# Five landing places instead of three for the second MLP's raw weights, and a later split of its first input block

## Chip, cores and metric

The program runs on one core of one Trainium2 chip. The metric is the device time of one execution in microseconds. Engines are named as in the profile: PE is TensorE (PEld its weight loads), DVE is VectorE, ACT is ScalarE, POOL is GpSimd, SP is SyncE, which issues all the transfers spoken of here.

## What is computed

Attention with a relative-position bias (four batches, eight heads, 576 positions, head dimension 64), then two MLPs on the resulting 2304 rows of 512:

```python
attn = softmax(q @ k.T / 8 + bias)                     # bias from a small MLP of the positions
x    = (attn @ v) as 2304 x 512
h    = max(x @ w1, x @ w2, x @ w3);  x = h @ w_out      # first MLP, hidden size 768
h    = x @ w_in                                         # second MLP, hidden size 2048
g    = h where h >= 1, 0 where h <= -1, (h + 1)**2 / 4 between
out  = g @ w_out
```

## The kernel before

Matrix products are made with each operand split into a high and a low fp16 part and three products of the parts. The program is one long Python loop; a scheduler at compile time puts each engine's instructions into a fixed order, by their place in the program and by when it thinks them ready. On the chip each engine then runs its list in order and waits where data isn't there. The same holds for SP's list of transfers.

The stretch of interest is the end of the attention and what follows it. At the end of the attention loop 45 units of the first MLP are still waiting in a list, `mlp_q` (L879, run at L1017): one last product of an earlier block (`mlp2`), then 18 `mlp1` and 4 `mlp2` of the block whose input lies in the tile "masks", then 18 `mlp1` and 4 `mlp2` of the last block, whose input lies in "xT". A unit `mlp1` (L800) is 12 matmuls (L808), a drain by ACT (L813) or DVE (L815), and for every third unit a split of the result by ACT (L819) and POOL (L820). A unit `mlp2` (L822) is 18 matmuls (L830), drains by ACT (L835) and a store to DRAM (L837). The first MLP's weights lie in `aw`, in the order in which the units use them: units 23 to 26 are the last to read its first 4096 columns.

Between these units stand the second MLP's raw weights: 32 pieces of 512 KB, each of which is loaded as it comes (L450), decoded into fp32 by ACT (L462, L463, L465) and DVE (L464), scaled by a maximum that PE helps to find (L549, L552), and split into two fp16 parts by ACT (L157) and DVE (L158) in its home. Pieces go by pairs; ten are done during the attention, the other 22 beside the 45 units, one pair for every four units (L1022). ACT's L462 or L463 is what reads a landing place last. A piece lands in one of three places in turn: before, `raws[0]`, `raws[1]` (the two halves of the first 2048 words of the tile `ws`) and `rt_` (the next 1024 words); from piece 12 on the first two are replaced by tiles named "v", of which there are two and which the attention also uses for its values. `load(2 * y + 2)` stands ahead of the decoding of pair y and `load(2 * y + 3)` behind it, in `late_pieces` (L556). The homes of the pieces are a list (L525); pieces 20 and 21 have theirs in "masks", so they wait for the block that reads it, pieces 22 to 26 in the last part of `ws`, 27 to 31 in tiles "k".

The second MLP takes its input in five blocks. `fetch_x2` (L851) brings a block into `qz`, `split_x2` (L855) finds its scale and splits it into one of two stores in turn, `x2_s` (L535): `ws`' first 4096 fp16 columns, which are `raws`, and `aw`'s first 4096. Block 0 is split behind unit 12 of `mlp_q`, counted from 0 (`PRM["xs"]`, L1019), block 1 during the second MLP's first block. That first block makes products L1056, results by ACT and DVE (L1069 to L1074) and products L1082, and needs the scales of all 32 pieces (`scales`, L1027). Beside it POOL combines weights for the later blocks (`wcomb`, L1111: L1120 to L1126, with ACT's L1125 between), which run with products L1134 and L1173 only.

Of the kernel before, what the change touches and what calls it, by code (L numbers as in the profile page):

```python
# [7 lines left out]
F16 = mybir.dt.float16  # L8
# [3 lines left out]
I64 = mybir.dt.int64  # L12
# [8 lines left out]
def kernel(ctx: ExitStack, tc: tile.TileContext, qt, kt, vr, small, mw1, mw2, mw3, mwo, win, wo2, out):  # L21
# [8 lines left out]
    P = 128  # L30
# [32 lines left out]
        group=16,  # L63
        look=4,
        xat=1,
        xs=12,
        bufs={'k': 5, 'pt': 4, 'xT': 2, 'phl': 4},
        xeng='vvvv',
        b1='vg',
# [23 lines left out]
    def st(shape, dt, tag):  # L93
        return sb.tile(shape, dt, tag=tag, name=tag, bufs=BUFS.get(tag, 1))
# [69 lines left out]
    if True:  # L164
# [361 lines left out]
        N_BIAS = 10  # L526
# [5 lines left out]
                home.append((st([P, S], F32, "k").bitcast(F16) if len(home) < 32 else st([P, 9, P], F16, "pt").rearrange("p c k -> p (c k)"))[:, :1024])  # L532
            return home[x]

        x2_s = [wss[:, 0:4], aws[:, 0:4]]  # L535
        n_late = [0]

        def late_to(n):
# [17 lines left out]
        def late_pieces():  # L556

            spec = []
            for ft in range(0, NF2, 2):
                spec.append([win[:, P * f:P * f + P].rearrange("(k p) f -> p k f", p=P) for f in (ft, ft + 1)])  # L560
                spec.append([wo2[P * f:P * f + P, :] for f in (ft, ft + 1)])

            spec = sum(spec, [])

            def load(x):
                if x >= len(spec):
                    return
                r = [raws[:, 0], raws[:, 1], rt_.rearrange("p a c -> p (a c)").bitcast(I64)][x % 3]
                if x >= N_BIAS + 2 and x % 3 < 2:
                    r = st([P, 10, 256], F16, "v").rearrange("p a c -> p (a c)")[:, 0:2048].bitcast(I64)  # L570
                loaded.append(raw_load(spec[x], r))

            loaded = []
            load(0)
            load(1)
            for y in range(len(spec) // 2):
                load(2 * y + 2)
                dst = [late_home(2 * y + i) for i in range(2)]
                zs = [decode(loaded[2 * y + i], st([P, S], F32, "sp")[:, :512].bitcast(U32), dst[i].bitcast(U32)) for i in range(2)]
                load(2 * y + 3)  # L580
                q = y // 2
                s = c_sq2[:, q:q + 1] if y % 2 else c_sp[:, 2 * q:2 * q + 2]
                pair_scale(s, [d.bitcast(U32) for d in dst], 12 if y % 2 else 14)
                for i in range(2):
                    split(dst[i][:, 0:512], dst[i][:, 512:1024], zs[i], s[:, 0:1] if y % 2 else s[:, i:i + 1], PENG[y % 2])
                yield
                yield
# [685 lines left out]
```

## Time and profile before

| | us |
|---|---|
| median of 3 runs | 1004.85 |
| lowest and highest | 1003.17, 1009.06 |
| the profiled execution | 1001.5 |
| its span (first to last instruction) | 999.6 |

The page gives the busy time of each engine over the span; the views used below are the busy time by stretches, the instructions of one engine in order of time, the waits of SP's queue, and the instructions of one line. In rows in order of time the bracket at the end gives the idle time just before the row and what ended it; "x12" is the number of instructions merged in the row.

### The profile page before, as it was taken

How to read it: one execution, taken by the hardware profiler on the slowest of the kernel's cores; microseconds unless marked ns; L12 is line 12 of the kernel's file. 1: busy time of each engine (PE TensorE's matmuls, PEld its weight loads, DVE VectorE, ACT ScalarE, POOL GpSimd, SP SyncE). 2: the span in 40 equal slices, each digit the busy share in tenths (PEclk: the TensorE clock that was granted, in tenths of full speed). 3: DMA queues.
4: the chain of work that ended last, by engine and by line, in shares of the span. 5: the costliest groups of instructions: out<-in, count | busy, mean ns of one | idle time of the engine just before them, and what ended most of it. 6: DMA issues, size and time to landing. Idle time of an engine off the chain costs nothing. (4 is left out here: it accounts for less than half of the span.)

```text
span 999.6 us, 25925 instructions
## 1 busy us (share of the span) xinstructions
PE 927.2 (93%) x10258; PEld 756.0 (76%) x10258; DVE 689.0 (69%) x1512; ACT 599.2 (60%) x1194; POOL 514.1 (51%) x734
## 2 busy tenths in 40 slices
PE   6768988899999999999899899999999999999996
PEld 5546777688888878778678778543688888888885
DVE  8998886767656686566454577876477586686565
ACT  3789875856665645778577698633444454454442
POOL 4133496748767755646367103995143344343442
PEclk8777979899999999999999999999999999999999
DMA  9996997997999879999989663010110010000000
GB/s 289 266 261 161 271 220 210 232 247 168 218 237 206 178 178 212 218 230 225 216 172 210 193 202 106 22 43 1 43 44 23 1 43 23 2 22 23 1 23 22
DMA packets 238969, 141.46 MB, mean 142 GB/s; under 512 B 187520, under 2 KB 217728, under 8 KB 238336
## 3 DMA queue, kind: packets, MB, share of 16 engines
q1 hardware_dynamic: 238688, 139.55, 58.6%
q8 instruction: 80, 1.31, 0.5%
q14 instruction: 41, 0.34, 0.1%
q10 hardware_dynamic: 160, 0.26, 0.1%
HBM read 79.68 MB, written 15.27 MB: 95 GB/s over the span
## 5 line engine op out<-in xcount | busy, mean ns | idle before, releaser
L808 PEld LDWEIGHTS <-aw 128*128 128x128 f16 x2160 | 190.1, 99 | 42.5 <-issue 20.0
L808 PE MATMUL pm<-xT,aw 128*128 128x256 f16 (+1 forms) x1812 | 201.9, 264 | 4.4 <-ACT hl L835 2.0
L731 POOL TENSOR_TENSOR phl<-sp,phl 128x512 f16<-128x512 f32 x136 | 162.2, 1193 | 0.0
L713 ACT ACTIVATE sp<-sp,mx 128x576 f32<-128x576 f32 x144 | 110.6, 769 | 67.8 <-DVE mx L711 67.3
L730 POOL TENSOR_TENSOR phl<-sp,phl 128x64 f16<-128x64 f32 x136 | 49.0, 360 | 189.6 <-ACT phl L729 157.1
L697 PE MATMUL s<-k,qz 64*128 64x288 f32 (+1 forms) x576 | 127.1, 459 | 15.1 <-DVE mx L711 9.8
L711 DVE CUSTOM_DVE_ANT_0 sp<-s,ab 128x576 f32<-128x576 f32 x128 | 93.2, 751 | 28.0 <-PE s L697 13.8
L1151 ACT ACTIVATE sp<-pm,vec 128x256 f32<-128x256 f32 x112 | 61.3, 555 | 80.0 <-PE pm L1134 77.2
L697 PEld LDWEIGHTS s<-k,qz 64*128 64x128 f32 (+1 forms) x576 | 69.0, 199 | 33.7 <-DVE mx L711 12.5
L729 ACT ACTIVATE phl<-sp 128x576 f16<-128x576 f32 x136 | 90.0, 673 | 4.8 <-DMA pt<-phl 4.1
L753 PEld LDWEIGHTS <-pt 128*128 128x128 f16 x1792 | 72.3, 100 | 25.5 <-DMA pt<-phl 14.4
L1155 POOL TENSOR_TENSOR hh<-hh 128x128 f32<-128x128 f32 x56 | 32.9, 588 | 106.4 <-DVE hh L1153 90.3
L1134 PEld LDWEIGHTS <-ab 128*128 128x128 f16 x756 | 73.8, 98 | 9.2
L753 PE MATMUL pav<-v,pt 128*128 128x64 f16 x1568 | 69.2, 195 | 9.0 <-DMA pt<-phl 8.9
L1152 DVE SCALAR_TENSOR_TENSOR hh<-pm,vec,sp 128x256 f32<-128x256 f32 x112 | 52.4, 477 | 32.3 <-ACT sp L1151 32.0
L820 POOL TENSOR_TENSOR hh<-hm,hh 128x256 f16<-128x256 f32 (+1 forms) x60 | 45.9, 766 | 52.4 <-ACT hh L819 52.3
L830 PE MATMUL pm<-hh,wo 128*128 128x256 f16 x558 | 70.3, 276 | 1.7 <-ACT hh L819 0.9
L830 PEld LDWEIGHTS <-wo 128*128 128x128 f16 x648 | 61.6, 99 | 13.1 <-issue 5.0
L815 DVE SCALAR_TENSOR_TENSOR hm<-pm,hm 128x256 f32<-128x256 f32 (+1 forms) x108 | 42.0, 389 | 33.7 <-PE pm L808 16.3
L1173 PEld LDWEIGHTS <-xT 128*128 128x128 f16 x588 | 57.4, 98 | 7.8 <-ACT xT L1160 1.2
L1173 PEld LDWEIGHTS <-wo 128*128 128x128 f16 x588 | 57.5, 98 | 6.7
L1156 POOL TENSOR_TENSOR hh<-hh 128x128 f32<-128x128 f32 x56 | 26.2, 468 | 68.4 <-DVE hh L1153 66.2
(298 smaller groups left out, 1986.1 us busy)
## 6 DMA issues: line engine op xcount, KB each, us to landing
k<-in_k_dram SPq DMA_DIRECT2D x64, 288.0 KB, 4.0
v<-v_d SPq DMA_DIRECT2D x24, 640.0 KB, 5.0
ws<-in_moe_w_out_dram SPq DMA_DIRECT2D x15, 512.0 KB, 5.1
ws<-in_moe_w_in_dram SPq DMA_DIRECT2D x9, 512.0 KB, 5.9
x_d<-hl SPq DMA_DIRECT2D x36, 128.0 KB, 2.6
qz<-in_q_dram SPq DMA_DIRECT2D x16, 256.0 KB, 4.4
ab<-in_moe_w_dram SPq DMA_DIRECT2D x8, 512.0 KB, 8.6
qz<-x_d SPq DMA_DIRECT2D x4, 1024.0 KB, 4.8
```

What stands on the lines that cost most here:

```text
L697: last_score[0] = T.matmul(sbox[i + r][:, c, :288], q[p, s if u.j == SJ else s // 2], k[p, 288 * c:288 * c + 288], start=True, stop=True)
L711: last_pair[0] = V.tensor_tensor_reduce(halves(sn), sbox.pop(i)[:, :, :288], halves(bias_sb[u.j][:, h]), -0.125, 3e38, ALU.add, ALU.min, mx)
L713: last_soft[0] = A.activation(pf, sn, AF.Exp, scale=-1.0, bias=mx, accum_out=u.sums[:, h:h + 1])
L729: A.activation(hl[:, :S], pf, AF.Copy)
L731: G.tensor_tensor(hl[:, S + 64:], pf[:, :512], hl[:, :512], ALU.subtract)
L753: T.matmul(u.pav[:, 64 * h:64 * h + 64], pt[:, c], v[:, sl, 64 * (h % 4):64 * (h % 4) + 64], **kw)
L808: T.matmul(o, wm[:, ft, i, wp, kk], x_rhs(key, xp, kk) if n == 256 else x_rhs(key, xp, kk)[:, c], start=(x == 0), stop=(x == 11))
L830: T.matmul(pm, wo16[:, ft, wp, P * d:P * d + P], hh[:, ft, hp], start=(ft == 0 and y == 0), stop=(ft == NF1 - 1 and y == 2))
L1134: T.matmul(pm, w[:, wp, kk], x2t[ORDER[y]][:, kk, xp, 256 * sub:256 * sub + 256], start=(x == 0), stop=(x == 11))
L1151: A.activation(r, pm, AF.Relu, scale=c_ch[:, f], bias=c_half)
L1152: V.scalar_tensor_tensor(t, pm, c_c[:, f], r, ALU.mult, ALU.max)
L1173: T.matmul(m[x], gl[:, gp, i], w[:, wp], start=(start and z == 0 and x % 2 == 0), stop=(stop and z == 2 and (x % 2 == 1 or x == 6)))
```

## The change

Three edits. The loads of raw weights are issued by `load_to(n)`, which issues all pieces below n that haven't been issued; from pair 5 on three pieces ahead of the pair that is decoded, at the pair before it already, and with five landing places in turn: `raws[0]`, a "v" tile, a "v" tile, `raws[1]`, `rt_`. The two stores of the second MLP's input blocks change places, so that block 0 goes to `aw` and block 1 to `ws`. Block 0 is split behind unit 32 of `mlp_q` instead of unit 12. The number of loads, decodings and splits and their sizes are the same.

```diff
@@ -63,7 +63,7 @@
-        xs=12,
+        xs=32,
@@ -532,7 +532,7 @@
-        x2_s = [wss[:, 0:4], aws[:, 0:4]]
+        x2_s = [aws[:, 0:4], wss[:, 0:4]]
@@ -562,22 +562,22 @@
-            def load(x):
-                if x >= len(spec):
-                    return
-                r = [raws[:, 0], raws[:, 1], rt_.rearrange("p a c -> p (a c)").bitcast(I64)][x % 3]
-                if x >= N_BIAS + 2 and x % 3 < 2:
-                    r = st([P, 10, 256], F16, "v").rearrange("p a c -> p (a c)")[:, 0:2048].bitcast(I64)
-                loaded.append(raw_load(spec[x], r))
+            def load_to(n):
+                while len(loaded) < min(n, len(spec)):
+                    x = len(loaded)
+                    r = [raws[:, 0], raws[:, 1], rt_.rearrange("p a c -> p (a c)").bitcast(I64)]
+                    r = r[x % 3] if x < N_BIAS + 2 else [r[0], None, None, r[1], r[2]][(x - N_BIAS - 2) % 5]
+                    if r is None:
+                        r = st([P, 10, 256], F16, "v").rearrange("p a c -> p (a c)")[:, 0:2048].bitcast(I64)
+                    loaded.append(raw_load(spec[x], r))
 
             loaded = []
-            load(0)
-            load(1)
+            load_to(2)
             for y in range(len(spec) // 2):
-                load(2 * y + 2)
+                load_to(2 * y + (5 if 2 * y >= N_BIAS else 3))
                 dst = [late_home(2 * y + i) for i in range(2)]
                 zs = [decode(loaded[2 * y + i], st([P, S], F32, "sp")[:, :512].bitcast(U32), dst[i].bitcast(U32)) for i in range(2)]
-                load(2 * y + 3)
+                load_to(2 * y + (5 if 2 * y + 2 >= N_BIAS else 4))
```

## Rows read from the trace of the kernel before

**Rows 1.** The page: the span, and busy time (share of the span) and instructions by engine.

```profile
span 999.6 us, 25925 instructions
PE 927.2 (93%) x10258; PEld 756.0 (76%) x10258; DVE 689.0 (69%) x1512; ACT 599.2 (60%) x1194; POOL 514.1 (51%) x734
```

**Rows 2.** Busy time by stretches: from:to, length, each engine's busy us, clock, DMA share, GB/s.

```profile
545.00:583.25 38.25, 34.32 (x379) 30.26 (x377) 20.02 (x55) 26.44 (x55) 5.82 (x8) 1.00 0.67 197
583.25:620.30 37.05, 33.15 (x321) 29.40 (x319) 27.44 (x66) 34.40 (x77) 5.05 (x6) 1.00 0.51 171
...
633.70:657.00 23.30, 23.30 (x111) 10.60 (x109) 19.35 (x24) 12.61 (x21) 22.91 (x19) 1.00 0.06 18
657.00:693.00 36.00, 32.42 (x148) 13.82 (x147) 23.17 (x22) 12.45 (x16) 32.03 (x27) 1.00 0.08 30
...
724.00:966.00 242.00, 242.00 (x2220) 216.90 (x2219) 169.83 (x348) 109.86 (x166) 102.33 (x198) 1.00 0.06 21
```

**Rows 3.** PE's instructions in order of time, 560 to 608 us: start, length, what.

```profile
560.99 0.38 PE L549 MATMUL s<-ab,ones 128*128 128x128 bf16 x4 [0.71 <-ACT ab L465]
564.29 2.78 PE L808 MATMUL s<-masks,aw 128*128 128x256 f16 x24 [0.52 <-ACT hm L813]
572.76 0.38 PE L549 MATMUL pm<-ab,ones 128*128 128x128 bf16 x4 [1.30 <-ACT ab L465]
581.94 1.47 PE L808 MATMUL s<-masks,aw 128*128 128x256 f16 x12
591.63 1.47 PE L808 MATMUL pm<-xT,aw 128*128 128x256 f16 x12 [0.97 <-ACT hl L835]
598.06 1.47 PE L808 MATMUL pm<-xT,aw 128*128 128x256 f16 x12 [1.03 <-ACT hl L835]
607.48 2.78 PE L808 MATMUL s<-xT,aw 128*128 128x256 f16 x24 [1.81 <-ACT hm L813]
```

**Rows 4.** ACT's instructions in order of time, 551 to 605 us.

```profile
551.46 0.66 ACT L462 ACTIVATE sp<-v 128x512 f32<-128x512 f32 x1 [2.49 <-DMA v<-in_moe_w_in_dram]
558.25 0.67 ACT L462 ACTIVATE sp<-v 128x512 f32<-128x512 f32 x1 [3.25 <-DMA v<-in_moe_w_in_dram]
574.93 0.68 ACT L463 ACTIVATE ab<-v 128x512 uint32<-128x512 uint32 x1 [1.71 <-DMA v<-in_moe_w_out_dram]
580.73 2.55 ACT L157 ACTIVATE ws<-qz,vec 128x512 f16<-128x512 f32 x4
604.44 0.67 ACT L463 ACTIVATE k<-v 128x512 uint32<-128x512 uint32 x1 [0.91 <-DMA v<-in_moe_w_out_dram]
```

**Rows 5.** SP's waits (us, times, longest), 545 to 620; L450's landing; one issue.

```profile
SPq L450 <- ACT sp L462: 21.4, 8, 5.9
SPq L853 <- DVE ws L158: 6.0, 1, 6.0
...
DMA to landing us min/median/max: 3.4/4.3/6.1
...
554.14 0.39 SPq L450 DMA_DIRECT2D v<-in_moe_w_in_dram  x1
```

**Rows 6.** L158 by shape, 540 to 700: duration ns min/median/max, starts.

```profile
L158 DVE SCALAR_TENSOR_TENSOR ws<-qz,vec,ws x4: 739/742/753, 581.5 to 584.5; 128x512 f16<-128x512 f32 x4
L158 DVE SCALAR_TENSOR_TENSOR aw<-qz,vec,aw x4: 1208/1213/1293, 649.6 to 666.8; 128x512 f16<-128x512 f32 x4
```

**Rows 7.** The second MLP's first result and its first use, DVE and PE by time.

```profile
632.45 1.03 DVE L1074 SCALAR_TENSOR_TENSOR phl<-sp,vec,phl 128x512 f16<-128x512 f32 x1 [0.79 <-ACT phl L1073]
638.84 1.89 PE L1082 MATMUL s<-ab,phl 128*128 128x512 f16 x8
```

**Rows 8.** POOL's combinations by time, and one wait of ACT for them.

```profile
620.46 0.73 POOL L1121 TENSOR_TENSOR xT<-xT 128x256 f32<-128x256 f32 x1 [4.53 <-issue]
655.22 2.12 POOL L1126 TENSOR_TENSOR aw<-xT,aw 128x1024 f16<-128x1024 f32 x1
671.98 1.06 ACT L1125 ACTIVATE aw<-xT 128x1024 f16<-128x1024 f32 x1 [3.71 <-POOL xT L1124]
```

## Prediction, made before the changed kernel was run

> **What bounds the kernel now.** I read the page first: the span is 999.6 us and TensorE (PE) is busy for 927.2 of it [rows 1]. So the question is where PE is idle in the stretch that the change touches, and nothing that another engine saves counts unless a PE gap closes. The view by stretches then shows four things [rows 2]. Between 545 us (the end of the attention) and 583.25 us PE is busy 34.32 of 38.25, so 3.93 us are lost. From there to 620.3 us, where the last product of the first MLP's first layer ends, it is busy 33.15 of 37.05: 3.90 us lost. From 657 to 693 us, inside the second MLP's first block, 32.42 of 36.00: 3.58 us lost. From 724 to 966 us PE is busy without a gap, so whatever is won earlier moves the rest of the program earlier by the same amount, and nothing more can be won there. The ceiling of the change is therefore 3.93 + 3.90 + 3.58 = 11.4 us.
>
> The PE rows give the long gaps one by one, with what ended each [rows 3]: 0.71, 0.52 and 1.30 us before 573 us, then 0.97, 1.03 and 1.81 between 590 and 608 us. All six end with an instruction of ScalarE (ACT): it had either not decoded a raw weight (L465), or not emptied a PSUM tile (L813, L835). ACT is an in-order queue that does both jobs, and its own rows show what it waited for [rows 4]: raw weights from DRAM, 2.49 us before 551.46, 3.25 before 558.25, 1.71 before 574.93 and 0.91 before 604.44, together 8.4 us. Those transfers were late because they had started late: the SyncE queue (SP), which issues them, held loads of L450 for 21.4 us in 8 waits, all on ACT's L462, the instruction that reads a landing place for the last time [rows 5]. A load needs 3.4 to 6.1 us to land, 4.3 in the median [rows 5]. So place, load and decoding form a loop: with three places, the load of an odd piece is issued only after the pair before it is decoded, and the next pair then stands behind a whole landing.
>
> **The change part by part.**
>
> *Five places.* No instruction is added or removed: the same loads and the same decoding, into other addresses. From piece 12 on the loads run three pieces ahead of the pair being decoded, where they ran one ahead. A landing of 4.3 us then has a whole pair's time to hide in, and in the two stretches from 545 to 620 us eleven pairs are worked on, one in some 7 us. So I take the DMA waits of ACT as nearly all gone, with one exception that no count of places cures: pieces 13 and 14 now land in the two attention tiles, and the second of those was given up only with the last attention product, by the SP row at 554.14 [rows 5].
>
> What PE gets of it is not 8.4 us. *Before 583 us* the three gaps of 0.71, 0.52 and 1.30 us [rows 3] stand behind ACT in the stretch in which ACT had 11.81 us idle (26.44 busy of 38.25) [rows 2]. I take them whole: 2.5 us. The other 1.4 us of this stretch, which no long row names, stay. *Between 583 and 620 us* ACT is busy 34.40 of 37.05 us [rows 2]; there the queue itself is nearly full, and its waits for data are a small part of it (0.91 us) [rows 4]. The price lies between 0 and 3.81 us, the sum of the three gaps there; I take half, 1.9 us. It is not nothing, because pairs that are done earlier take work out of this stretch: pieces 20 and 21 may not be decoded until the products on the tile "masks" (their later home) are over, at 583.4 us [rows 3], but pieces 22 and 23 have another home, and with two more places they can be loaded and decoded ahead of that.
>
> *The later split.* The split of the first input block moves from after unit 12 of the queue of remaining units to after unit 32. It is 4 ACT instructions, 2.55 us in one run [rows 4], and 4 on VectorE (DVE), 0.742 us each [rows 6]; with it move eight small DVE steps and one small product (for the block's scale), and behind it the fetch of the second block into qz. In the old place it ran at 580.7 us, when ACT had to wait for "masks" anyway. In the new one it falls between 583 and 620 us: 34.40 + 2.55 = 36.95 us of ACT work for 37.05 us, which is why I don't take more than half above. Its result is wanted by the first product of the second MLP, after the end of the first MLP's first layer at 620.3 us, and there PE has that MLP's second layer to fill in with. How much delay is hidden further on can be read off: the first block's first result is ready when the DVE step at 632.45 ends, at 633.5, and PE uses it at 638.84 [rows 7]; 5.3 us of cover. So a delay of 2.55 us at the end costs nothing, one of 8 us costs 2.7.
>
> If the split slipped past 620 us it would meet GpSimd (POOL), which is then busy nearly without a pause, 22.91 of 23.30 us [rows 2]. The same four DVE instructions for the second block, which do run there, took 1.213 us each instead of 0.742 [rows 6]: 4 x 0.47 = 1.9 us more, under the cover of 5.3. The Trainium skill is harsher ("SBUF — State Buffer", section "Who interferes with whom"): a DVE instruction with two SBUF inputs and a GpSimd instruction that reads SBUF exclude each other for the whole instruction. By that rule each of the four could wait out one of POOL's; the longest there take 2.12 us [rows 8], so it would be a loss of 8.5 us less the cover, 3.2 us. The rows at 1.213 us speak for the milder form; I keep the harsher one as a rival.
>
> *Swapped homes of the input blocks.* The first block goes to the first 4096 columns of aw, read last by unit 26, six units before the split; the second goes to the old landing places, all decoded before the first block's results can be made (633.5 us, above), while the second split's DVE steps run from 649.6 us [rows 6]. Both waits are over before. Nothing.
>
> *The stretch from 657 to 693 us.* Its gaps come from ACT waiting behind POOL's combinations: 3.71 us ahead of one L1125 alone, with L1073 queued behind it [rows 8]. POOL starts that chain when the last product of the first layer is over, at 620.46, so it moves with PE, and the distance between them stays. I take 0; the bounds are 3.58 us gained, and the same lost if ACT's order falls worse.
>
> **The sum.** 2.5 + 1.9 + 0 = 4.4 us. The profiled run took 1001.5 us (1.9 outside its span), so it would take 997.1. It was a quick one: the three timed runs had a median of 1004.85, and 1004.85 - 4.4 = 1000.4 is the forecast.
>
> **The rivals.**
>
> *All gaps close* (0.16). ACT gets ahead early enough that the gaps between 583 and 608 us close and stage 657 to 693 us closes in part too: 7 to 11.4 us, 993.5 to 997.9. For it: all six long gaps end with ACT. Against: ACT's 93% in the second stretch.
>
> *The change does nothing that counts* (0.26). The waits for data vanish and ACT waits for something else (the "masks" gate, its own queue filled by the moved split): between 2 us gained and 3 lost, 1003 to 1008, 1004.9 in the middle. For it: 36.95 of 37.05 us.
>
> *The fetch blocks the loads* (0.12). This one ends slower. SP is in order, and in the kernel before it already waited 6.0 us at L853 for the split's last DVE step before it issued the fetch of the second block, with loads behind it [rows 5]. When the split stands later, the compiler's order may put this fetch among the last loads and the stores of the first MLP's results. If SP waits there for a split that ACT reaches late, the 6.0 us come on top, once, with nothing won: 1004.85 + 6.0 = 1010.9. It decides from the point where the pieces already landed are used up: at most three pieces, so about one pair and a half or 10 us of lead in place of none; a longer wait is needed than I expect, and hence the low chance.
>
> *POOL excludes the moved split* (0.03): the harsher form above, 4.4 - 3.2 = 1.2 us gained, 1003.7.
>
> The forecast has the rest, 0.43, with 2 to 7 us gained: 997.9 to 1002.9.
>
> **How the numbers follow.** A measurement of this kernel can tell about 0.5% from no change, 5.0 us. Faster by more than that (under 999.8) are the case of all gaps, 0.16, and some three fifths of the forecast's range, 0.26, since the median that I start from lies above the profiled run: 0.42. Slower by more (over 1009.9) is most of the blocked fetch and the tail of the case without effect: 0.12. The rest is 0.46. The range goes from the lower end of the best case, 993.5, to the upper end of the case without effect, 1008; it leaves out the blocked fetch and a little at either side.
>
> **What the profile after would show.** If I am right, SP's waits at L450 on ACT's L462 fall well under 21.4 us, ACT's waits for raw weights nearly vanish before 583 us, the PE gaps at L549 are gone, and the split's rows read aw between 600 and 620 us. PE still has 1 to 3 us of gaps after 583 us, now with ACT busy through them. If ACT is idle in front of the products on "masks" and PE's loss between 583 and 620 us is the same or greater, the case without effect is the right one. If SP shows a long wait at L853 with loads of L450 or stores of L837 behind it, the blocked fetch is. The prediction is wrong in its base if the stretch from 657 to 693 us changes by more than 2 us either way, since I gave it nothing.

## The result, and the profile after

The changed kernel takes 1016.45 us (median of 6 runs, 1014.5 to 1019.02), the kernel before, timed beside it, 1006.35 (6 runs, 1002.31 to 1009.06): a ratio of 1.0097, 95% interval 1.0073 to 1.0121. The change costs 1%, some 10 us, where 4.4 us were forecast as a gain. The profiled run took 1016.11 us.

The page and the view by stretches of the kernel after; columns as in [rows 1] and [rows 2]. The stretches hold the same work as those of [rows 2] and lie later: the end of the attention to the last product on "masks", from there to the last product of the first layer, and the part of the second MLP's first block that lost time.

```profile
span 1014.3 us, 25931 instructions
PE 942.2 (93%) x10258; PEld 766.9 (76%) x10258; DVE 688.0 (68%) x1512; ACT 598.4 (59%) x1194; POOL 514.2 (51%) x734
...
551.60:592.90 41.30, 34.97 (x374) 30.38 (x373) 20.03 (x50) 27.02 (x56) 6.83 (x9) 0.96 0.70 200
592.90:633.90 41.00, 36.41 (x331) 31.43 (x330) 28.09 (x71) 33.62 (x75) 5.60 (x6) 0.96 0.39 129
669.90:705.90 36.00, 30.83 (x141) 13.19 (x139) 23.33 (x22) 12.45 (x16) 31.88 (x27) 1.00 0.08 30
```

PE is idle for 6.33, 4.59 and 5.17 us in them, where it was 3.93, 3.90 and 3.58 [rows 2]: every stretch is worse. In two of them the clock is granted at 0.96 in the mean, where it was 1.00. ACT isn't fuller than before: 33.62 of 41.00 us in the second, where it was 34.40 of 37.05. The engine that was to be relieved is idle for longer.

PE's instructions in order of time in the kernel after, the same view as [rows 3]:

```profile
571.17 2.81 PE L808 MATMUL s<-masks,aw 128*128 128x256 f16 x24 [1.68 <-ACT hm L813]
586.42 4.06 PE L808 MATMUL s<-masks,aw 128*128 128x256 f16 x24 [3.22 <-ACT hm L813]
610.77 2.78 PE L808 MATMUL s<-xT,aw 128*128 128x256 f16 x24 [1.09 <-DVE hm L815]
616.16 0.22 PE L248 MATMUL pm<-btmp,ones 128*128 128x128 bf16 x1 [2.61 <-ACT hm L813]
616.43 2.72 PE L808 MATMUL s<-xT,aw 128*128 128x256 f16 x12
```

The short gaps at L549 of [rows 3] are gone, as forecast. In their place stand longer ones, 1.68, 3.22 and 2.61 us, all three until ACT's drain L813, and one of 1.09 us until DVE's drain L815. Behind the two longest the next 12 products take 2.72 in place of 1.47 us (24 take 4.06 in place of 2.81): 1.25 us more. The gap of 2.61 us ends at L248, the small product for the scale of the moved split.

ACT's instructions ahead of the gap of 3.22 us, and the loads of SP at that time:

```profile
576.73 1.24 ACT L462 ACTIVATE sp<-ws 128x512 f32<-128x512 f32 x2
577.85 0.39 ACT L813 ACTIVATE hm<-pm 128x256 f32<-128x256 f32 x1
578.11 0.43 ACT L819 ACTIVATE hh<-hm 128x256 f16<-128x256 f32 x1
578.48 1.23 ACT L465 ACTIVATE ab<-sp 128x512 bf16<-128x512 f32 x2
583.04 0.66 ACT L463 ACTIVATE ws<-ws 128x512 uint32<-128x512 uint32 x1 [3.33 <-DMA ws<-in_moe_w_out_dram]
583.60 0.40 ACT L819 ACTIVATE hh<-hm 128x256 f16<-128x256 f32 x1
583.91 1.32 ACT L157 ACTIVATE ab<-sp,vec 128x512 f16<-128x512 f32 x2
585.43 0.67 ACT L462 ACTIVATE sp<-v 128x512 f32<-128x512 f32 x1 [0.20 <-DVE ab L158]
586.00 0.37 ACT L813 ACTIVATE hm<-s 128x256 f32<-128x256 f32 x1
...
572.83 4.98 SPq L450 DMA_DIRECT2D ws<-in_moe_w_in_dram  x2
577.99 0.37 SPq L450 DMA_DIRECT2D ws<-in_moe_w_out_dram  x1
```

This is the place to learn from. The instruction at 583.04 decodes piece 22, the first whose home is the tile ws. With five places in turn, piece 22 lands where piece 17 lay. ACT reads piece 17 for the last time in the pair of L462 at 576.73; the load goes out at 577.99, as soon as the place is free; ACT stands before it from 579.7 and waits until 583.04, 5.1 us after the issue. The drain at 586.00, for which PE waits, stands behind it in ACT's list. Pieces 20 and 21 were asked for ahead of it (the two loads at 572.83), but may not be decoded until "masks" is free, so they hold two of the five places. In the kernel before, the load of piece 22 went out at 578.91 and its decoding came at 584.41 without a wait, and between the two ACT did the four splits at 580.73 [rows 4]. SP's and ACT's rows of the kernel before:

```profile
578.91 0.34 SPq L450 DMA_DIRECT2D v<-in_moe_w_out_dram  x1
...
584.41 0.66 ACT L463 ACTIVATE ws<-v 128x512 uint32<-128x512 uint32 x1
```

SP's waits for 549 to 626 us in the kernel after, columns as in [rows 5]:

```profile
SPq L853 <- DVE tcol L137: 12.3, 1, 12.3
SPq L450 <- ACT sp L462: 11.1, 7, 4.1
SPq L450 <- ACT hm L813: 9.0, 3, 7.9
...
SPq L450 <- ACT masks L463: 6.9, 1, 6.9
```

The wait of the loads on L462 halves, from 21.4 us [rows 5] to 11.1, as forecast. A part of it comes back under other names: 6.9 us on L463, which [rows 5]' view doesn't have for "masks", and 9.0 on L813, where the kernel before has this:

```profile
SPq L450 <- ACT hm L813: 5.8, 1, 5.8
```

**From where the times are counted.** The part ahead of the change scatters: the last score product of the attention (L697) starts at 539.7 us in the profiled run of the kernel before, at 546.3 in that after, and at 550.0 in a run further down whose lists are the same as before but for the names of four tiles. From that product to the end, though, this last run and the kernel before agree within 0.2 us (459.7 and 459.9), and so do the changed kernel and depth_undone, whose lists are the same too (468.0 and 467.8). So in the table all times are counted from the start of the last L697. The first five columns are starts or ends of groups of PE's rows, "end" is the span less the start of that product.

| run | last product on "masks" | first on "xT" | last on "xT" | first L1082 | first L1134 | end |
|---|---|---|---|---|---|---|
| before | 43.4 | 51.9 | 80.3 | 99.1 | 171.0 | 459.9 |
| after | 46.6 | 52.3 | 87.6 | 105.4 | 178.9 | 468.0 |
| split_only | 44.3 | 50.4 | 88.3 | 108.4 | 183.1 | 472.0 |
| five_places_split_early | 47.9 | 55.9 | 85.9 | 102.7 | 177.6 | 466.5 |
| split_early_late_decode_of_22 | 42.6 | 51.8 | 81.5 | 98.0 | 171.0 | 460.0 |
| late_decode_of_piece_22 | 42.2 | 49.6 | 82.0 | 99.2 | 174.1 | 463.1 |
| scale_early | 45.2 | 53.8 | 85.0 | 101.7 | 174.3 | 463.6 |
| three_places_scale_early | 43.5 | 52.8 | 84.9 | 104.5 | 178.4 | 467.4 |

After loses 3.2 us up to the last product on "masks" (46.6 against 43.4), 4.1 more up to the last on "xT" (87.6 - 80.3 = 7.3), and 0.8 more up to the end: 8.1 of the 10 us.

### The profile page after: what moved, and what is told of

It is laid out like the page before. It is cut to its first block, busy times and chain, and to the rows that moved or that the text cites. A ratio compares the mean times of both kernels' runs of the same rounds, so it can differ in the third digit from the quotient of the medians.

```text
span 1014.3 us, 25931 instructions
## 1 busy us (share of the span) xinstructions
PE 942.2 (93%) x10258; PEld 766.9 (76%) x10258; DVE 688.0 (68%) x1512; ACT 598.4 (59%) x1194; POOL 514.2 (51%) x734
## 5 line engine op out<-in xcount | busy, mean ns | idle before, releaser
L697 PE MATMUL s<-k,qz 64*128 64x288 f32 (+1 forms) x576 | 133.2, 469 | 10.5 <-DVE mx L711 7.4
L753 PEld LDWEIGHTS <-pt 128*128 128x128 f16 x1792 | 75.2, 103 | 29.0 <-DMA pt<-phl 16.6
L697 PEld LDWEIGHTS s<-k,qz 64*128 64x128 f32 (+1 forms) x576 | 72.6, 205 | 30.0 <-DVE mx L711 9.6
L753 PE MATMUL pav<-v,pt 128*128 128x64 f16 x1568 | 72.3, 199 | 10.7 <-DMA pt<-phl 10.4
L1134 PEld LDWEIGHTS <-ab 128*128 128x128 f16 x756 | 73.8, 98 | 9.2
L830 PEld LDWEIGHTS <-wo 128*128 128x128 f16 x648 | 61.1, 98 | 13.0 <-issue 5.8
L830 PE MATMUL pm<-hh,wo 128*128 128x256 f16 x522 | 64.6, 273 | 1.6 <-ACT hh L819 0.9
L815 DVE SCALAR_TENSOR_TENSOR hm<-pm,hm 128x256 f32<-128x256 f32 (+1 forms) x106 | 41.2, 389 | 34.3 <-PE pm L808 19.8
```

What stands on the lines that cost most here:

```text
L697: last_score[0] = T.matmul(sbox[i + r][:, c, :288], q[p, s if u.j == SJ else s // 2], k[p, 288 * c:288 * c + 288], start=True, stop=True)
L753: T.matmul(u.pav[:, 64 * h:64 * h + 64], pt[:, c], v[:, sl, 64 * (h % 4):64 * (h % 4) + 64], **kw)
L830: T.matmul(pm, wo16[:, ft, wp, P * d:P * d + P], hh[:, ft, hp], start=(ft == 0 and y == 0), stop=(ft == NF1 - 1 and y == 2))
L1134: T.matmul(pm, w[:, wp, kk], x2t[ORDER[y]][:, kk, xp, 256 * sub:256 * sub + 256], start=(x == 0), stop=(x == 11))
```

## The experiments

All ratios are to the kernel before, timed in the same batch, with 95% intervals.

| run | median us | ratio | interval |
|---|---|---|---|
| split_only | 1019.86 | 1.0113 | 1.0066 to 1.0160 |
| depth_undone | 1016.02 | 1.0082 | 1.0051 to 1.0113 |
| places_first_as_before | 1019.33 | 1.0100 | 1.0066 to 1.0133 |
| five_places_more_decode_tiles | 1008.74 | 1.0000 | 0.9974 to 1.0027 |
| before_more_decode_tiles | 1013.84 | 1.0080 | 1.0051 to 1.0108 |
| scale_early | 1010.57 | 1.0035 | 1.0013 to 1.0057 |
| three_places_scale_early | 1013.49 | 1.0068 | 1.0031 to 1.0104 |
| split_after_unit_40 | 1015.34 | 1.0076 | 1.0043 to 1.0109 |
| five_places_more_tiles_scale_early | 1007.00 | 1.0002 | 0.9975 to 1.0028 |
| stores_on_scalar_queue | 1017.88 | 1.0110 | 1.0075 to 1.0146 |
| scale_early_stores_on_scalar | 1012.43 | 1.0043 | 1.0025 to 1.0062 |
| tiles_scale_stores | 1009.44 | 1.0026 | 1.0003 to 1.0049 |
| split_early_in_own_tiles | 1008.88 | 1.0002 | 0.9979 to 1.0024 |
| five_places_split_early | 1014.96 | 1.0071 | 1.0044 to 1.0097 |
| scale_early_no_split | 1016.00 | 1.0061 | 1.0032 to 1.0090 |
| three_places_no_split | 1012.01 | 1.0036 | 1.0017 to 1.0056 |
| late_decode_of_piece_22 | 1014.86 | 1.0074 | 1.0048 to 1.0100 |
| split_early_late_decode_of_22 | 1007.51 | 1.0003 | 0.9979 to 1.0027 |

### Which of the edits

The first runs take the change apart. split_only is the kernel before with the two edits of the split alone:

```diff
-        xs=12,
+        xs=32,
-        x2_s = [wss[:, 0:4], aws[:, 0:4]]
+        x2_s = [aws[:, 0:4], wss[:, 0:4]]
```

> The three landing places and the loads of before; only the split stands behind unit 32 and the two stores of the input blocks are swapped. Theory A (the moved split is what costs: the gaps of 1.09 and 2.61 us of TensorE at 610 to 616 us of the changed kernel, with the slow clock after them): ratio 1.005 to 1.010. Theory B (the five places are what costs: pieces decoded out of turn, ScalarE waiting for data ahead of drains, gaps of 1.68 and 3.22 us at 569 to 586 us, and the loads beside the last attention tiles): ratio 0.998 to 1.003 here.

depth_undone is the changed kernel with the loads asked for as late as before:

```diff
-                load_to(2 * y + (5 if 2 * y >= N_BIAS else 3))
+                load_to(2 * y + 3)
-                load_to(2 * y + (5 if 2 * y + 2 >= N_BIAS else 4))
+                load_to(2 * y + 4)
```

> Five places and the later split as in the changed kernel, but each load is asked for where the kernel before asked for it (one piece ahead of the pair, the next behind the decoding). The compiler's lists for SyncE, ScalarE and TensorE come out the same as the changed kernel's, entry for entry. All theories therefore expect the changed kernel's time: ratio to before 1.010, 1014 to 1019 us, and the profile tells how much of the 4.35 us that the changed kernel was behind at 477 us, before any difference in the lists, is scatter: then it should differ here by some us again.

places_first_as_before uses the five places in another turn, and asks for the first of them a pair later. In it piece 14 lands where piece 11 still lies, so that piece 11's weights are decoded from other data; the work is the same.

```diff
-[r[0], None, None, r[1], r[2]][(x - N_BIAS - 2) % 5]
+[None, None, r[2], r[0], r[1]][(x - N_BIAS - 2) % 5]
-                load_to(2 * y + (5 if 2 * y + 2 >= N_BIAS else 4))
+                load_to(2 * y + (5 if 2 * y >= N_BIAS else 4))
```

> The changed kernel with the five places in another turn: pieces 12 and 13 to the v tiles and 14 to the third place, as in the kernel before, 15 and 16 to the first two. So no raw weight of piece 12 is loaded during the attention and 14 does not wait for the last attention product. If the loads beside the attention's end are a third of the loss (theory B, first half: some 3.5 us by the two traces between 477 and 563 us), ratio 1.005 to 1.007; if the split alone costs (A), 1.010 as the changed kernel.

The later split alone costs 1.13%: no part of the forecast had a price for it. Its two edits, the later place and the other home, were not run apart. The depth at which the loads are asked for has no effect that the timing can tell, and the compiler's lists for PE, ACT and SP are the same with it and without: what counts is when a place is free. The turn of the places doesn't matter either, within the intervals. Two gaps of split_only, PE's rows:

```profile
587.05 2.78 PE L808 MATMUL s<-masks,aw 128*128 128x256 f16 x24 [3.04 <-ACT hm L813]
...
617.99 2.72 PE L808 MATMUL s<-xT,aw 128*128 128x256 f16 x12 [4.29 <-ACT hm L813]
```

and what ACT did ahead of the second:

```profile
613.67 0.66 ACT L463 ACTIVATE k<-v 128x512 uint32<-128x512 uint32 x1 [2.56 <-DMA v<-in_moe_w_out_dram]
...
617.58 0.36 ACT L813 ACTIVATE hm<-s 128x256 f32<-128x256 f32 x1
```

The drain came 3.9 us after ACT had resumed from a wait for a load of 2.56 us, with six other steps between, decodings and a split of a result. That is the same picture as in the changed kernel, with three places. The load that ACT waits for goes out behind four stores in a row:

```profile
601.12 6.42 SPq L837 DMA_DIRECT2D x_d<-hl  x4
607.78 0.33 SPq L450 DMA_DIRECT2D v<-in_moe_w_out_dram  x1
```

From 1.0113 alone I read at first that the loss was the split's and that the places gained a little (1.0113 to 1.0097). The runs with the early split, further down, show that the places lose by themselves.

### The scale of the moved split

The small product L248 has its place in PE's list between products of the first layer, and the eight small DVE steps stand between drains. These runs make the scale behind unit 12 as before, and leave only the four splits behind unit 32, with five places and with three; a third moves everything to unit 40.

```diff
-        def split_x2(y):
+        def x2_scale(y):
...
+            if x == 12:
+                x2_scale(0)
             if x == PRM["xs"]:
                 x2_done(split_x2(0))
```

> The changed kernel, but the scale of the first input block (its maximum over partitions with one small TensorE product, and the eight small VectorE steps) is made behind unit 12, where the kernel before had it; only the four splits by ScalarE and VectorE stay behind unit 32. Theory A1: the moved part that hurts is the chain TensorE to VectorE to ScalarE of the scale, which stands in the in-order lists among the last block's drains (gap of 2.61 us in front of that product, ScalarE's and VectorE's waits behind it): ratio 1.000 to 1.004, and the last block's first layer (35.3 us from its first to its last product in the changed kernel, 28.4 before) comes down to under 31 us. Theory A2: the splits' 2.55 us of ScalarE, or the reordered transfers, hurt: 1.007 to 1.012 and over 33 us.

> Three landing places and their loads as in the kernel before, the split behind unit 32, its scale behind unit 12. Against the run with the scale early and five places (1.0035), this shows what the five places are worth by themselves when the scale is out of the way; against the run with only the split moved (1.0113), what the scale's place is worth with three places. If the five places do nothing: 1.002 to 1.005. If they gain what I forecast (some 4 us): 1.006 to 1.009.

> The changed kernel with the split behind unit 40, the last unit of the last block's first layer. Theory A (split and scale among the drains of that layer): the layer is freed of it, under 31 us from first to last product instead of 35.3, and what is lost is only what the first products of the second MLP wait for: ratio 1.002 to 1.006. Theory D (the loads: with the split gone from unit 12 the compiler puts four stores in a row ahead of the loads of the last pieces, which then land late at ScalarE): the stretch stays over 33 us and the ratio at 1.008 to 1.012.

With five places the early scale gives back 0.62% (1.0097 to 1.0035), 6.2 us; with three 0.45% (1.0113 to 1.0068), 4.5 us, though there the two intervals overlap. In scale_early the gap at the scale's product is gone, but one of 2.01 us stays close by:

```profile
616.33 1.47 PE L808 MATMUL s<-xT,aw 128*128 128x256 f16 x12 [2.01 <-ACT hm L813]
```

The gap of 3.22 us at "masks" is gone too, though ACT waits for piece 22 even longer there, 4.16 us:

```profile
582.24 0.67 ACT L463 ACTIVATE ws<-ws 128x512 uint32<-128x512 uint32 x1 [4.16 <-DMA ws<-in_moe_w_out_dram]
...
584.87 2.81 PE L808 MATMUL s<-masks,aw 128*128 128x256 f16 x24 [0.51 <-DVE tcol L249]
```

PE's list holds other products ahead of that point here, among them the scale's and the first ones of L830, and shorter gaps follow (1.12 and 0.76 us). What a wait of ACT costs depends on what PE still has to do in it. So a part of the later split's price goes with its scale, which I had counted as "eight small DVE steps and one small product" and priced at nothing; how much of that is the product's own place and how much the other order isn't shown. Unit 40 is no better than 32, within the intervals.

The two pairs with the later split also compare five places with three, and there five look better: by 0.16% with the late scale (1.0113 to 1.0097) and by 0.33% with the early one (1.0068 to 1.0035). The intervals overlap in both pairs, but the profiles, counted from the last L697, say the same, 4.0 us (472.0 to 468.0) and 3.8 us (467.4 to 463.6). By these rows what the places are worth depends on where the split stands; the timed runs alone don't show the gain.

### SP's queue

In the changed kernel the four stores of the block in "masks" stand on SP ahead of loads. Here ACT issues them.

```diff
-            SP.dma_start(x2_d[key[0]][:, d, 256 * key[1]:256 * key[1] + 256], t)
+            (A if key[0] == SJ else SP).dma_start(x2_d[key[0]][:, d, 256 * key[1]:256 * key[1] + 256], t)
```

> The changed kernel, with the four stores of the block on the masks tile issued by ScalarE instead of SyncE; the other lists stay nearly the same. In the changed kernel SyncE stands 6.98 us at those four stores before it issues the load whose landing ScalarE then waits for (1.12 us, with the drains behind it and gaps of 1.09 and 2.61 us on TensorE). If this blocking is the cause of those gaps (theory D): ScalarE's wait gone, the last block's first layer from 35.3 to under 33 us, ratio 1.005 to 1.008. If the gaps come from the scale's chain and the order on ScalarE (A1): over 34 us and 1.008 to 1.011.

> Scale behind unit 12 and stores on ScalarE's queue, five places, split behind unit 32. If both causes are real and add up, 2 to 3 us less than with the scale early alone (1.0035): 1.000 to 1.002. If the stores have no part: 1.002 to 1.005.

Neither is faster than its partner (1.0110 against 1.0097, 1.0043 against 1.0035): with five places the stores aren't what the loads cost. With three, where the load of the 2.56 us wait goes out right behind them, this wasn't run.

### Tiles for the decoded values

A decoding also needs one of four tiles "sp". These runs take idle "pt" tiles for every second pair from piece 14 on, with the change, without it, and with the other edits.

```diff
-st([P, S], F32, "sp")[:, :512].bitcast(U32)
+(st([P, S], F32, "sp")[:, :512].bitcast(U32) if y < 6 or y % 2 == 0 else st([P, 9, P], F16, "pt").rearrange("p c k -> p (c k)")[:, :1024].bitcast(U32))
```

> The changed kernel, with the decoded fp32 pieces of every second pair from pair 7 on in the four attention tiles named pt, which are idle by then, instead of the four tiles named sp: twice the tiles. Theory C: a landing place is freed by L462, which needs a free sp tile, so the places were never what loads waited for, and five of them free nothing. If C holds, the waits of SyncE's loads on L462 shrink to under half of the changed kernel's 11 us, ScalarE's waits for data fall from 14 to under 7 us and the ratio to 0.998 to 1.005. If C does not hold, 1.008 to 1.012.

> The kernel before with only the decoded pieces of every second pair from pair 7 on in the idle pt tiles. Theory C (the four sp tiles hold up L462 and with it the landing places): faster, ratio 0.993 to 0.998, SyncE's waits at L450 on L462 down from 21.4 to under 12 us. If the three landing places are the limit once the tiles are not, ratio 0.998 to 1.002 and the waits stay.

> The changed kernel with both edits: more tiles for decoded pieces, and the first block's scale made behind unit 12. If the two causes (A1 and C) add up, 6 to 8 us from the tiles and 6 to 9 us from the scale come off the changed kernel's 10 us loss: ratio 0.993 to 0.998, faster than the kernel before. If the scale has no part, 0.998 to 1.002 as with the tiles alone.

> All three repairs on the changed kernel: more tiles for decoded pieces, scale behind unit 12, the four stores on ScalarE's queue. The version that might beat both: 0.995 to 0.999 if the stores were holding loads there too; 0.999 to 1.002 if not.

With them the changed kernel is back at 1.0000, but the kernel before gets slower by 0.8%, so tiles as such are not what was short. The trace suggests more. ACT's rows of five_places_more_decode_tiles:

```profile
580.50 0.66 ACT L463 ACTIVATE ws<-v 128x512 uint32<-128x512 uint32 x1
581.58 0.37 ACT L813 ACTIVATE hm<-pm 128x256 f32<-128x256 f32 x1
581.84 0.67 ACT L463 ACTIVATE ws<-v 128x512 uint32<-128x512 uint32 x1
583.81 0.66 ACT L463 ACTIVATE ws<-ws 128x512 uint32<-128x512 uint32 x1
```

Here the compiler has put piece 22 (ws<-ws) behind two other pieces and a drain, and ACT doesn't wait for it at all. That suggested the last test. Early scale or moved stores add nothing to this.

### The places alone

With the split left behind unit 12, block 0 can't go to ws, where two of the five places are. It goes to the four tiles "pt", which the attention no longer uses; first with three places, as a yardstick, then with five.

```diff
+            if y == 0:
+                x2t[j] = InPt([st([P, 9, P], F16, "pt").rearrange("p c k -> p (c k)")[:, :1024].rearrange("p (s t) -> p s t", s=2) for d in range(KK)])
```

> The kernel before, with three places and the split behind unit 12, but with the first input block's four parts written to the four "pt" tiles, which the attention no longer uses, in place of the first columns of ws. Nothing else moves. It is the yardstick for the next run: both theories expect 1.000 (within 0.3%). If it is slower, the "pt" tiles carry a price of their own, and the next run has to be read against this one.

> Five places as in the change, but the scale and the split of the first block stay behind unit 12; the block goes to the "pt" tiles, so that the places in ws stay free. Theory S (the places gain 2 to 3 us, and the whole loss comes with the later split): ratio 0.996 to 0.999 to the kernel before, and the last block's first layer takes about 28 us from its first to its last product, as in the kernel before. Theory L (any change of the order of the decodings costs, the places as much as the split): 1.003 to 1.010, with gaps behind ScalarE's drains between 570 and 620 us as in the changed kernel.

The yardstick is exact (1.0002). Five places without the later split cost 0.71%, the interval 0.44 to 0.97%: here they gain nothing, and the theory that the loss is all the split's falls. PE, ACT and SP of five_places_split_early:

```profile
587.04 2.72 PE L808 MATMUL s<-masks,aw 128*128 128x256 f16 x12 [2.85 <-DVE hm L815]
...
578.65 0.68 ACT L463 ACTIVATE ws<-ws 128x512 uint32<-128x512 uint32 x1 [3.66 <-DMA ws<-in_moe_w_out_dram]
...
584.49 2.54 ACT L157 ACTIVATE pt<-qz,vec 128x512 f16<-128x512 f32 x4
...
573.27 0.37 SPq L450 DMA_DIRECT2D ws<-in_moe_w_out_dram  x1
```

It is piece 22 again: issued at 573.27, and waited for until 578.65 (5.4 us) ahead of the drains and of the four splits, which stood in that time in the kernel before.

### The four splits left out

Without them the second MLP's first block is made from whatever lies in aw.

> Five places, scale of the first block made behind unit 12, its four splits behind unit 32 left out (the second MLP reads what lies in aw, so its first block isn't the reference's). Against scale_early (1.0035) it measures what the four splits themselves cost. If the remaining 3.5 us are theirs: 0.999 to 1.001. If they lie in the order of decodings and drains: 1.003 again.

> The same with three places: scale early, the four splits left out (the first block isn't the reference's). Against three_places_scale_early (1.0068). If the four late splits cost those 7 us: 1.000. If most of it is that without a split behind unit 12 the compiler puts decodings ahead of the first MLP's drains there, it stays at 1.004 to 1.007.

```diff
+                    if y:
                       split(x2t[j][:, d, 0], x2t[j][:, d, 1], x[:, d], c_sx[:, j:j + 1], XENG[d])
```

With three places 0.32% go (1.0068 to 1.0036), with five the time rises by 0.26% (1.0035 to 1.0061), both within overlapping intervals. Leaving work out changed the order of the rest: with five places a drain now stands earlier among the decodings, and PE's worst gap is 3.06 us in another place, with three 3.68 us. So the price of the four splits by themselves stays open. With five places the kernel with less work isn't the faster one.

### One decoding moved behind the drains

The decisive pair. The compiler is told to put the decoding of pieces 22 and 23 behind the last drain of the block in "masks"; nothing else in the source is changed. The compiler then puts other instructions elsewhere too: against the kernel without the edit the lists differ, with the early split, at 185 of PE's 10258 places and 61 of ACT's 1194, with the late one at 124 and 50.

```diff
+                with tc.issue_after(drain[0].ins) if y in (11,) else nullcontext():
                     zs = [decode(loaded[2 * y + i], st([P, S], F32, "sp")[:, :512].bitcast(U32), dst[i].bitcast(U32)) for i in range(2)]
```

> The same edit in five_places_split_early (1.0071), where L463 ws<-ws waits 3.66 us and TensorE's gap is 2.85 us with 12 products at the half clock behind it. Theory W: 2.85 + 1.25 = 4.1 us less, about 1.003. Rival: 1.006 to 1.008 with the wait at another decoding.

> The changed kernel, but the decoding of pieces 22 and 23 (the pair behind the two whose home is "masks") may stand in ScalarE's list only behind the last drain of the block that reads "masks". In the changed kernel L463 ws<-ws stands ahead of those drains and waits 3.33 us for its load, and TensorE has a gap of 3.22 us behind it and 12 more products at the half clock (24 in 4.06 in place of 2.81 us). Theory W (that is where a part of the loss comes from): 3.2 + 1.25 = 4.5 us less, 1.0097 to 1.005, and the gap of 3.22 us is gone. Rival (the wait only shows that loads are late there; moved behind, something else waits as long): 1.009 to 1.011, and the wait for a load of about 3 us stands at another decoding, with a TensorE gap of 2 us or more.

With the early split the whole loss is gone: 1.0071 (1.0044 to 1.0097) becomes 1.0003 (0.9979 to 1.0027). ACT and PE of that run:

```profile
585.81 2.56 ACT L157 ACTIVATE pt<-qz,vec 128x512 f16<-128x512 f32 x4
...
589.34 0.37 ACT L813 ACTIVATE hm<-s 128x256 f32<-128x256 f32 x1
589.61 0.67 ACT L463 ACTIVATE ws<-ws 128x512 uint32<-128x512 uint32 x1
...
587.29 1.47 PE L808 MATMUL s<-masks,aw 128*128 128x256 f16 x12
```

The decoding runs behind the splits and the last drain and doesn't wait, and the last 12 products on "masks", which had the gap of 2.85 us before them and took 2.72, have no gap and the full clock: 1.47 us. In the table 5.3 us of the 6.5 that are won lie ahead of the end of these products (47.9 to 42.6, and 466.5 to 460.0 at the end). The gap and the slow products make 4.1 us; the rest goes with the other order. A second gap of five_places_split_early, 2.55 us at 613.10 with 24 products in 4.45 us behind it, is 0.87 us in the pinned run, and gaps of 1.46 and 1.48 us stand in new places.

With the late split the gap of 3.22 us goes too (0.73 us is left), and in the table the last product on "masks" comes 4.4 us earlier (46.6 to 42.2). The timed ratio moves less, from 1.0097 to 1.0074, and the intervals overlap; the profiled run ends 4.9 us earlier (468.0 to 463.1). What is left there is mostly this:

```profile
613.49 1.47 PE L808 MATMUL s<-xT,aw 128*128 128x256 f16 x12 [2.67 <-ACT hm L813]
```

It stands at the same products as the gap at the scale in the changed kernel.

## Why the prediction was wrong

**The base.** PE sets the time, and the longest gaps of the changed kernel (3.22, 2.61 and 1.68 us) end with ACT: right. Not every one does: its gap of 1.09 us ends with DVE's drain, and so does that of 2.85 us in five_places_split_early. The three stretches were the right ones to look at.

**"A landing of 4.3 us then has a whole pair's time to hide in."** This step failed, and with it the term of 4.4 us. ACT's waits of over 0.9 us for loads were to vanish nearly; they were five before, 2.07 (at 548.29, which my rows left out) and the four of [rows 4], 10.4 us in all, and are six after (1.70, 1.96, 3.40, 1.26, 3.33 and 1.12), 12.8 us. The first of them, in the kernel before:

```profile
548.29 0.68 ACT L463 ACTIVATE ab<-ws 128x512 uint32<-128x512 uint32 x1 [2.07 <-DMA ws<-in_moe_w_out_dram]
```

Counting places isn't enough. Two pieces that are loaded but locked (20 and 21, until "masks" is free) take two places out of the turn, so that the next piece is loaded when the place of a piece just decoded comes free, as with three. And ACT's list isn't in the order of the pieces: with five places the compiler takes piece 22 ahead of the locked ones and ahead of the drains, where its load has had no time. I had written that pieces 22 and 23 could be "loaded and decoded ahead of that", and counted it as a gain. For piece 22 it was none: the kernel before loads it at 578.91 and already takes it ahead of the locked ones, at 584.41, but behind the last drain of the block. Of the early waits the longest, 3.40 us, is that for the attention's second tile, the exception I named, and that of 1.26 us is for piece 17. The other two are for the loads at 548.85 and 549.33, which go out among the attention's transposes, 6.3 and 8.4 us before ACT could go on (555.12 and 557.75):

```profile
548.85 0.44 SPq L450 DMA_DIRECT2D ws<-in_moe_w_out_dram  x1
549.33 0.43 SPq L450 DMA_DIRECT2D ws<-in_moe_w_in_dram  x1
...
555.12 0.66 ACT L463 ACTIVATE ab<-ws 128x512 uint32<-128x512 uint32 x1 [1.70 <-DMA ws<-in_moe_w_out_dram]
557.75 0.67 ACT L463 ACTIVATE ab<-ws 128x512 uint32<-128x512 uint32 x1 [1.96 <-DMA ws<-in_moe_w_in_dram]
...
566.19 0.68 ACT L463 ACTIVATE ab<-v 128x512 uint32<-128x512 uint32 x1 [3.40 <-DMA v<-in_moe_w_out_dram]
```

With the split early and the one bad place mended, five places are worth 0 (1.0003), not 4.4 us. The 4.0 and 3.8 us by which the profiles put them ahead of three places with the late split come near the forecast in size only: the kernels that they are counted against are slower than the kernel before.

**"A delay of 2.55 us at the end costs nothing."** This failed too: alone, with three places, it costs 11.4 us (1.0113). I looked for its price at its new place and at the one consumer of its result, where there was cover. I had seen that in the old place it ran when ACT "had to wait" anyway, and drew only that its time there was free. The runs show that the order around it changed: drains stand behind waits for loads, 3.04 and 4.29 us of PE's gaps in split_only. Whether the split had been filler that kept decodings from moving up ahead of the drains is my reading and isn't shown: in five_places_split_early the split stands early, and piece 22 is taken ahead of the drains all the same. Its scale isn't nothing: moved back it gives 6.2 us with five places, and 4.5 with three, where the intervals overlap. The sum of 36.95 us of ACT work for 37.05 didn't come to decide anything: ACT had 7.4 us idle in that stretch (33.62 of 41.00).

**The moved steps themselves.** Their sizes held: ACT's four took 2.55 us at 617.85, DVE's 740 to 744 ns from 620.0 on, ahead of the end of the first layer (633.9), as forecast. The rival by the harsher form of "SBUF — State Buffer" ("Who interferes with whom", the Trainium skill) had next to no chance to cost anything there; POOL's combinations began at 634.34. One POOL instruction, which reads SBUF, did run beside them, if POOL's spans are taken as they stand:

```profile
619.99 1.40 DVE L158 SCALAR_TENSOR_TENSOR aw<-qz,vec,aw 128x512 f16<-128x512 f32 x2
...
620.79 1.13 POOL L820 TENSOR_TENSOR hh<-hm,hh 128x256 f16<-128x256 f32 x1 [2.10 <-ACT hh L819]
```

DVE's second step had begun first, ran until 621.39 and wasn't longer; POOL's instruction, begun at 620.79, took 1.13 us, where the one at 618.02 took 0.67. That is what the rule would give if POOL waited for DVE, and a milder form would give it too: one pair of rows, on an engine whose spans are rough, doesn't decide between the two.

**The blocked fetch.** A part of its sign came, a wait of 12.3 us at L853, and its price didn't: the fetch goes out at 623.53, behind all the loads, the last of them in the row at 608.32, and only four stores stand behind it, at 643.22. A long wait in a queue counts for what stands behind it. The slower side came by another way than my rival for it.

**657 to 693 us.** 5.17 us are lost there in place of 3.58, 1.6 us, inside the 2 us that I had allowed.

**The sign.** The case in which ACT "waits for something else" was the nearest of the rivals in its mechanism, and its upper end of 3 us of loss was too low by 7 (the blocked fetch, 1010.9, was nearer in its number alone): I bounded the loss by the work that moves (2.55 us), not by what the order of three in-order lists can do with it.

**What adds up, and what doesn't.** Places alone cost 0.71%, the later split alone 1.13%, both together 0.97%: they aren't terms of a sum, since both act through the same list of ACT. Of the 10 us of the change, the decoding of piece 22 is 2.3 us by the timed runs, whose intervals overlap, and 4.9 by the profile, the late scale 6.2 us by the timed runs and 4.4 by the profile (468.0 to 463.6). The two mends were not run together, and since the early scale alone closes the gap of 3.22 us too, they needn't add up. It stays open what the four splits alone are worth, what in the new order costs the rest of the later split's price, and why the pinned kernel with the late split is slower by 7 us in the timed runs (1010.5 to 1018.37 us, the profiled one 1011.66) but by 3.2 in its profile (463.1 against 459.9).

None of these kernels beats the kernel before; the best are level with it.

## What to carry to other kernels

More landing places helped here only as far as the piece that is decoded next had been asked for longer ago than a landing takes: before adding places, go through the turn by hand, see which pieces are locked by a gate, and ask when the place of the next one comes free. Where one in-order engine both decodes and empties PSUM, price a moved or enabled step by which drains will stand behind a wait, not by its own duration; a step that seems to run in idle time may be what keeps a wait from standing there. If the loss sits at one instruction, pinning that one behind the work that others wait for is a cheap test, and the lists before and after tell what else the scheduler moved with it.

## What the hardware showed that I hadn't expected

After each PE gap of some 2.6 us or more in this stretch of the changed kernel the granted clock fell to the lower level (1.2 GHz) for about 12 products, 2.72 us in place of 1.47, so that a gap of 3.22 us cost 4.5. The gap's length alone doesn't decide: split_only ran at full clock behind a gap of 3.04 us (24 products in 2.78 us), and late_decode_of_piece_22 behind one of 2.67 us (12 in 1.47), while scale_early took 4.29 us for 24 products behind one of 2.00. The rows don't settle what decides it. The mean clock of two short windows of the changed kernel, the columns as above:

```profile
580.00:590.00 10.00, 6.78 (x56) 5.43 (x54) 4.36 (x12) 5.32 (x11) 0.67 (x1) 0.83 0.46 160
...
615.00:620.00 5.00, 3.78 (x23) 2.86 (x23) 2.21 (x12) 4.40 (x10) 0.67 (x1) 0.66 0.01 6
```
